# Where the transposes of a cosine attention and mixer kernel are made: DMA queue or TensorE

## The chip, the core and the metric

The kernel runs on one core of a Trainium2 chip. Its engines are TensorE (PE, matmuls; PEld is its weight load), VectorE (DVE), ScalarE (ACT), GpSimd (POOL) and SyncE (SP); 16 DMA engines serve the queues that SP and POOL issue to. The metric is the device time of one execution in microseconds (us); lower is better. The kernel before took 548.46 us (median of 3 runs, 548.42 to 548.52).

## The reference: what is computed

Attention with normalised queries and keys over 8 batches of 12 heads, 448 positions and 64 dimensions a head, and on its result a mixer with a low-rank step and a wide MLP:

```python
q_n = q / (norm(q) + 1e-06); k_n = k / (norm(k) + 1e-06)
attn = softmax(q_n @ k_n.T / tau)          # per batch and head
x = (attn @ v), heads joined               # [8, 448, 768]
u = x + (x.T @ U @ V).T                    # U [448, 32], V [32, 448]
out = u + relu(u @ w_ch1) @ w_ch2          # w_ch1 [768, 3072], w_ch2 [3072, 768]
```

## The kernel before, in words

**Order of the work.** The program first lists all work as `Op`s: engine, planned duration, what it depends on, which buffer slots it takes (`acq`) and gives back (`rel`). `Plan.run` then simulates the engines with these durations and sorts all operations by their planned start. Every engine executes its instructions in that fixed order on the chip; nothing is reordered there. PE's operations stand in streams with a rank: of the streams whose next operation is ready, the first listed one goes (transposes `pe_tp` before attention products `pe_av`, scores `pe_sc` after them, and the MLP `pe_mlp` last, as what fills PE). An operation of PE is planned only 0.1 us (`SEM`) and a margin (`plan.safe`: 0.2 us while batch 1 is listed, 0.5 us for batches 2 to 7) after the end of what it depends on. A DMA on the queue of SP is planned as 0.1 us of issue, its work on one shared line ("x"; 1.0 us for a store of u) and a fixed delay (2.0 us for it). `"ACT/DVE"` means that whichever of the two is free takes the operation.

**Attention.** For each batch b = 0 to 7 and each of 6 head pairs, q and k come in by POOL's queue, are squared and summed (`squares`, L641 to L649), and scaled on DVE (`norm`, L717) into a tile `xn` of 112 rows with 8 blocks of 128 columns (4 of k, 4 of q, two heads side by side). The scores need each block transposed, `qkT`, in the tile that the profile calls sqk. In batches 0 and 1 (`PE_BATCHES = 2`) the function `flip` (L559 to L580) does that on PE: transposes with `ident` (the matmul at L571) into one PSUM bank, then one copy to SBUF by ACT (L1446) or DVE (L1448). In batches 2 to 7 one DMA transpose for the pair, issued by SP (L733), takes the place of both. Scores (L781) follow in bursts of three slots that take pairs of the PSUM banks 0 to 5, exponentials on ACT (L799), products with v (L826), and a scaling on DVE (L857, L858) into X, of which there are two buffers, one for the even and one for the odd batches. `LAST` says at which pair the scores of the last 64 keys of pairs 0, 2 and 4 (and of the pair after each) are made in batches 2 to 7.

**u.** `stage0` projects X with U (L941), multiplies with V (L994) and adds that to X in place (L1003). Two batches together make seven tiles of 128 rows, named (z, t) with z = b // 2; tile t = 3 holds 64 rows of each batch, so each batch makes its half of it. A store on SP's queue (L1032) writes each tile to DRAM, `kept[x]`. For batch 0's tiles and tile (0, 3) the columns (the transposed u, which the MLP needs) are made on PE and never leave the chip.

**The MLP.** `mlp` handles the first four tiles. The other 24 go in twelve host pairs: `columns_of` fetches for each tile the columns into the single buffer `uT` by a DMA transpose of `kept[x]` (L891) and the rows by a plain load (L895). `mlp_seven` then multiplies: the first six pairs at L1270 (up) and L1299 (down), the last six at L1163 (up, with sums of weights that L1122 to L1125 write into buffers which attention no longer needs, X among them) and L1299. Where the plan leaves PE idle for over 0.25 us, filler matmuls go in (L703).

Lines of note: `flip` L559, matmul L571; `squares` L627; `norm` with L733; `stage0` with L1032; `columns_of` with L891 and L895; copies of `copy_op` L1446 (ACT) and L1448 (DVE).

Of the kernel before, what the change touches and what calls it, by code (L numbers as in the profile page):

```python
# [317 lines left out]
def kernel(  # L318
# [31 lines left out]
    HALF = 6  # L350
    POOL_XN = {}
    WHOLE = 3
    LAST = {0: 0, 2: 2, 4: 5}
    WIDE = 1
    TB = 2
    RAW_KEYS = {(0, 0), (0, 1)}
# [48 lines left out]
    r_ur = Shrink([u_t[:, i, :] for i in range(3)], 3, (0, 1))  # L405
    dram = ctx.enter_context(tc.tile_pool(name="dram", bufs=1, space=bass.MemoryType.DRAM))
    kept = {(z, t): dram.tile([128, C], BF, name=f"u_{z}_{t}") for z in range(B // 2) for t in range(7) if (z, t) >= (0, 3)}
    uT_t = const.tile([128, CC * 512], BF, name="uT")
    r_uT = fixed_ring([uT_t])

# [53 lines left out]
    r_z = bank_ring([(7,), (4,), (6,), (5,), (3,), (1,), (2,), (0,)], 4)  # L464
    r_sc = bank_ring([(0, 1), (2, 3), (4, 5)], 3)
    r_low = bank_ring([(5,), (4,), (3,), (2,), (1,), (0,)], 4)
    r_av3 = bank_ring([(5,), (4,), (3,), (2,), (1,), (0,)], 2, (4, D + 8))
    r_av2 = bank_ring([(5,), (4,), (3,), (2,), (1,), (0,), (6,)], 2, (4, D + 8))
    r_up0 = bank_ring([(7,), (6,), (5,), (4,), (3,), (2,), (1,), (0,)], 3)
# [32 lines left out]
    pe_first = plan.stream("PE")  # L502
    pe_z2 = plan.stream("PE")
    pe_z1 = plan.stream("PE")
    pe_av = plan.stream("PE")
    pe_z0 = plan.stream("PE")
    pe_a = plan.stream("PE")
# [14 lines left out]
    def dve_t(n, fast=1, fixed=0.065):  # L522
        return fixed + n * 0.00105 / fast
# [32 lines left out]
            in_=moe_w_ch2.rearrange("(a p) c -> p a c", p=128)[:, i * w:(i + 1) * w, :]),  # L556
            C * w * 128 * 4 / 415e3)

    def flip(stream, ins, n, into, part, deps, acq, rel, wide=1, eng="ACT/DVE", took=0.05):  # L559


        tp = Slot(r_mm, 1)
        tp.own = True
        for z, x in enumerate(ins):
            def fn(z=z, x=x):
                if z == 0:
                    w = len(ins) // wide
                    tp.tile = bank_t[:, tp.group[0], :].bitcast(BF)[:, 0:w * n].rearrange(
                        "p (w n) -> p w n", w=w)
                m = 128 // wide  # L570
                nc.tensor.transpose(out=tp.tile[m * (z % wide):m * (z % wide + 1), z // wide, :], in_=x(),  # L571
                                    identity=ident[:n, :n])
            o = plan.add(Op("PE", took, fn, deps=deps + [id_set] if z == 0 else (), acq=[tp] + acq,
                            rel=rel if z == len(ins) - 1 else []), stream)
        took = any_t(n * len(ins) // wide, 2)
        c = plan.add(Op(eng, took, None, deps=[o], acq=acq, rel=[tp], prio=0.2, fast=True))

        def move():
            for dst, src in part(into(), tp.tile):
                copy_op(c, dst, src)  # L580
        c.fn = move
        return c
# [45 lines left out]
    def squares(b, g, ld, ops, lo, ii, ss, pr, on, hold, then):  # L628

        red = []  # L630
        for i in ii:
            for a0 in range(0, g, G // 2):
                a1 = min(g, a0 + G // 2)
                sq = Slot(r_sq, 1)
                o = Op(on, 1.02 if on == "POOL" else {"ACT": 0.52, "DVE": 0.34} if "/" in on else 0.52 if on == "ACT" else 0.34, None,
                       deps=[ops[i], *hold], acq=[sq], prio=pr + 0.2, fast=True, port=True)

                def square(o=o, i=i, a0=a0, a1=a1, sq=sq):
                    x, y = ld.tile[:, i, lo + a0:lo + a1, :], sq.tile[:, 0:a1 - a0, :]
                    if o.by == "ACT":  # L640
                        nc.scalar.activation(out=y, in_=x, func=AF.Square)  # L641
                    elif o.by == "POOL":
                        nc.gpsimd.tensor_mul(y, x, x)  # L643
                    else:
                        nc.vector.tensor_mul(y, x, x)
                o.fn = square
                plan.add(o, pool_q if on == "POOL" else None)
                red.append(plan.add(Op("DVE", dve_t(256 * (a1 - a0)),
                    lambda i=i, a0=a0, a1=a1, sq=sq: nc.vector.reduce_sum(  # L649
                        ss.tile[:, i, a0:a1, :].rearrange("p h c -> p (h c)"),  # L650
                        sq.tile[:, 0:a1 - a0, :].rearrange("p h (c d) -> p (h c) d", d=D),
                        axis=AX.X),
                    deps=[o, *then], acq=[ss], rel=[sq], prio=pr + 0.1)))
        return red
# [50 lines left out]
    def norm(b, p, ld, la, inv, a, deps, pr, loaded):  # L705


        by_pe = b < PE_BATCHES
        first = b == 0 and p == 0
        xn, qkT = Slot(r_xn, 2 if by_pe and (first or (b, p) not in RAW_KEYS) else 1), Slot(r_qkT, SC if b == 0 else sum(p in members(b, x) for x in groups_of(b)))  # L710

        def part(i):
            def fn():
                src = ld.tile[:, i, la:la + 2, :].rearrange("p h (c d) -> p h c d", d=D)
                sc = inv.tile[:, i, a:a + 2, :].unsqueeze(3).to_broadcast([SCH, 2, SC, D])
                dst = xn.tile[:, SC * (1 - i):SC * (2 - i), :].rearrange("p c (h d) -> p h c d", h=2)
                (nc.gpsimd if pool_ else nc.vector).tensor_mul(dst, src, sc)  # L717
            pool_ = i in POOL_XN.get(b, ())
            return plan.add(Op("POOL" if pool_ else "DVE", 1.05 if pool_ else dve_t(512), fn, deps=[deps[i]], acq=[xn],
                               rel=[getattr(ld, "slot", ld), inv], prio=pr, port=True), pool_x if pool_ else None)  # L720

        def raw():
            c = Op("ACT/DVE", any_t(512), None, deps=loaded[1], acq=[xn], rel=[ld.slot], prio=-0.9)
            c.fn = lambda: copy_op(
                c, xn.tile[:, 0:SC, :].rearrange("p c (h d) -> p h c d", h=2),
                ld.tile[:, 1, la:la + 2, :].rearrange("p h (c d) -> p h c d", d=D))
            return plan.add(c)

        keys = (b, p) in RAW_KEYS
        ops = {0: part(0), 1: raw()} if first and keys else {0: part(0)} if keys else {  # L730
            i: part(i) for i in ((0, 1) if first else (1, 0))}
        if not by_pe:
            done = [plan.add(Op("SP", 0.1, lambda: nc.sync.dma_start_transpose(  # L733
                out=qkT.tile, in_=xn.tile.rearrange("p b e -> p (b e)")), deps=list(ops.values()), acq=[qkT],
                rel=[xn], prio=0, lat=("x", 0.05 * 56, 5.0)))]
        else:
            done = []
            for i in (1, 0) if keys else ops:
                b0, b1 = SC * (1 - i), SC * (2 - i)
                ins = [(lambda z=z: xn.tile[:, z, :]) for z in range(b0, b1)] if i in ops else [  # L740
                    (lambda c=c, hh=hh: ld.tile[:, 1, la + hh, D * c:D * c + D]) for c in range(SC) for hh in range(2)]
                done.append(flip(
                    pe_tp, ins, SCH,
                    lambda: qkT.tile, (lambda t_, x, b0=b0, b1=b1: [(t_[:, b0:b1, :], x)]),
                    [ops[i]] if i in ops else loaded[1], [qkT], [xn if i in ops else ld], len(ins) // SC,
                    "ACT/DVE", 0.05))
        got[b, p, "qkT"] = (qkT, done, (inv, a, deps[1]))
        return list(ops.values())
# [123 lines left out]


    prev, first_v, made, u_adds, projects = {}, {}, {}, {}, {}

    class Columns:

# [7 lines left out]
    def columns_of(tiles, uses=NC * CC, given=None):  # L885
# [2 lines left out]
        us = []  # L888
        for i, x in enumerate(tiles):
            if given is None:  # L890
                ut.append(plan.add(Op("SP", 0.1, lambda i=i, x=x: nc.sync.dma_start_transpose(  # L891
                    out=uT.tile[:, :, i * 128:(i + 1) * 128], in_=kept[x]),
                    deps=made[x], acq=[uT.slot], prio=0, lat=("x", 0.05 * 48, 2.0))))
            u = Slot(r_ur, 2)
            u.back = plan.add(Op("SP", 0.1, lambda x=x, u=u: nc.sync.dma_start(out=u.tile, in_=kept[x]),  # L895
                                 deps=made[x], acq=[u], prio=1, lat=("x", 1.0, 2.0)))
            us.append(u)
# [31 lines left out]
    def stage0(b, X, muls):  # L929
# [95 lines left out]
        for i, t in enumerate(tiles):  # L1025
# [5 lines left out]
            made.setdefault(x, []).append(plan.add(Op(  # L1031
                "SP", 0.1, lambda x=x, r=r, t=t: nc.sync.dma_start(out=kept[x][r, :], in_=X.tile[r, t - 3 * par, :]),  # L1032
                deps=u_adds[x], rel=[X], prio=1 if b == 1 else 0, lat=("x", 1.0, 2.0))))
        prev["A"], prev["X"] = A, X
        return us, uT, ut

# [563 lines left out]
    for n in range(0, len(rest), 2):  # L1600
        if n // 2 == HALF:
            up = seven_rows([hosts[-1][0][-1]], [
                [o for t in range(4) for o in made[3, t][:1]]] * 2 + [
                [o for p in range(NPAIR) for o in got[B - 1, p, "qkT"][1]] if i in (2, 4) else
                [last_av[B - 1 if i == 6 else B - 2, p] for p in range(NPAIR)] for i in range(2, 7)])
            held = stores + [last_av[B - 1, p] for p in range(NPAIR)]
# [54 lines left out]
```

## Time and profile before

| what | value |
|---|---|
| median of 3 runs | 548.46 us |
| the profiled execution's own time | 547.75 us |
| its span, first to last instruction | 546.0 us |
| PE busy | 537.7 us, 98% |
| DVE busy | 448.7 us, 82% |
| ACT busy | 280.7 us, 51% |
| POOL busy | 141.8 us, 26% |
| DMA transposes of q and k (L733) | 36, 4.5 us from issue to landing (median) |
| DMA transposes of u (L891) | 24, 3.3 us |
| stores of u (L1032) | 28, 2.6 us |
| matmuls at L571 (transposes on PE) | 106 |

How to read the views that the prediction uses: the busy slices divide the span in 40 equal parts, a digit is the busy share in tenths, and PEclk is TensorE's granted clock in tenths. The chain of work that ended last, in order of time, has the start in us, the length in us, and the engine, tile and line, with the number of instructions. The waits have the waiting engine, tile and line, what released it, and then the total in us, the number of times and the longest. A row of the timeline begins with the start and the length in us of a group of like instructions that lie together. A row of one source line has the durations in ns (least, median, most) and the first and last start. The windows have, for a stretch, the busy us of each engine. The duration of a matmul runs from its start to its modelled end and overlaps the next one; the distance between the starts of two neighbours is called the pitch here.

### The profile page before, as it was taken

Reading aid. Unit: us, or ns where it says so; the run is one execution under the profiler, and the core shown is the slowest. Engines: PE = TensorE matmul, PEld = TensorE weight load, DVE = VectorE, ACT = ScalarE, POOL = GpSimd, SP = SyncE. Lnnn points to the kernel's source line nnn. Section 1 sums busy time; section 2 is a strip of 40 time slices with the busy share of each in tenths; the row PEclk is TensorE's granted clock in tenths of the full one; section 3 lists DMA queues with packets and bytes.
Section 4 is the critical chain, followed back from the end, with each engine's and each line's share of the span. In section 5 each row is a group of like instructions: output and inputs, shape, how many; then the busy total and the mean of one; then the engine's idle time right before and its main releaser. Section 6 shows DMA issues by size and latency. Waiting matters only on the chain.

```text
span 546.0 us, 15182 instructions
## 1 busy us (share of the span) xinstructions
PE 537.7 (98%) x6276; PEld 390.2 (71%) x6276; DVE 448.7 (82%) x1033; ACT 280.7 (51%) x459; POOL 141.8 (26%) x180
## 2 busy tenths in 40 slices
PE   8899999999999999999999999999999999999996
PEld 7565655677757857767757857868778787878783
DVE  8979949999899989979979976678968585858583
ACT  7977646466456746766765664732323231314140
POOL 8636233100711611631631610010202020111111
PEclk9999999999999999999999999999999999999999
DMA  9999999941985987998996975023041312122301
GB/s 156 202 207 141 206 203 159 199 88 47 140 190 102 121 140 145 135 141 136 137 154 102 133 138 92 32 53 87 16 139 30 88 32 88 30 88 32 88 1 59
DMA packets 142325, 61.11 MB, mean 112 GB/s; under 512 B 101008, under 2 KB 142256, under 8 KB 142256
## 3 DMA queue, kind: packets, MB, share of 16 engines
q0 software_dynamic: 72352, 25.73, 44.3%
q1 hardware_dynamic: 69904, 34.41, 29.1%
q8 instruction: 49, 0.80, 0.6%
q14 instruction: 20, 0.16, 0.1%
HBM read 56.93 MB, written 15.93 MB: 133 GB/s over the span
## 4 chain that ended last, share of the span: by engine, by line
PE 94%; DVE 3%; ACT 1%; POOL 1%; DMA 1%; issue 0%; DVEq 0%; POOLq 0%
PE bank L1299 30%; PE bank L1270 18%; PE bank L1163 15%; PE bank L826 8%; PE bank L781 7%; PE bank L1382 6%; PE bank L1424 6%; PE bank L994 2%; DVE qk_all L717 1%; PE bank L941 1%; DVE ss L649 1%; POOL sqk L643 1%; DMA relu<-in_q_dram 1%; PE bank L571 1%; DVE X_sb L864 0%; ACT attn L794 0%
## 5 line engine op out<-in xcount | busy, mean ns | idle before, releaser
L799 ACT ACTIVATE attn<-bank 128x896 bf16<-128x896 f32 (+1 forms) x163 | 139.1, 915 | 39.9 <-PE bank L781 34.0
L1299 PEld LDWEIGHTS <-relu 128*128 128x128 bf16 x1008 | 96.0, 98 | 67.1 <-issue 7.2
L1270 PE MATMUL bank<-uT,w_sb 128*128 128x256 bf16 x864 | 103.9, 273 | 0.0
L1299 PE MATMUL bank<-w_sb,relu 128*128 128x384 bf16 x576 | 101.9, 326 | 0.0
L1270 PEld LDWEIGHTS <-w_sb 128*128 128x128 bf16 x864 | 81.8, 98 | 18.7 <-issue 8.2
L649 DVE TENSOR_REDUCE ss<-sqk 112x8 f32<-112x512 bf16 x96 | 62.5, 676 | 2.7 <-ACT sqk L641 2.0
L717 DVE TENSOR_TENSOR qk_all<-qk_all,inv 112x512 bf16<-112x512 bf16 x93 | 60.7, 682 | 0.8 <-DMA sqk<-qk_all 0.5
L826 PEld LDWEIGHTS <-attn 128*128 128x128 bf16 (+1 forms) x1536 | 54.3, 97 | 6.6 <-issue 2.9
L593 POOL DMA_DIRECT2D qk_all<-in_q_dram x24 | 17.7, 736 | 155.4 <-ACT attn L799 76.9
L826 PE MATMUL bank<-v_nat,attn 128*128 128x65 bf16 (+1 forms) x1536 | 57.3, 193 | 0.6 <-DVE X_sb L864 0.6
L1163 PEld LDWEIGHTS <-w_sb 128*128 128x128 bf16 x864 | 49.3, 98 | 0.8
L1280 ACT ACTIVATE relu<-bank 128x512 bf16<-128x512 f32 x45 | 26.9, 597 | 42.2 <-PE bank L1270 42.0
L1200 ACT COPY attn<-bank 128x512 f32<-128x512 f32 x18 | 10.5, 587 | 74.1 <-PE bank L1163 73.2
L781 PE MATMUL bank<-sqk 64*64 64x448 bf16 (+1 forms) x460 | 46.9, 356 | 0.7 <-ACT sqk L1446 0.5
L1163 PE MATMUL bank<-uT,w_sb 128*128 128x128 bf16 x648 | 38.1, 219 | 0.0
L1191 ACT ACTIVATE relu<-relu 128x512 bf16<-128x512 bf16 x36 | 22.6, 630 | 29.9 <-DVE relu L1185 29.1
L616 POOL DMA_DIRECT2D v_nat<-in_v_dram x42 | 31.2, 759 | 18.6 <-DMA w_sb<-in_moe_w_ch_dram 14.9
L1382 PE MATMUL bank<-uT,w_sb 128*128 128x384 bf16 (+1 forms) x288 | 35.9, 273 | 0.0
L1424 PE MATMUL bank<-w_sb,relu 128*128 128x384 bf16 x192 | 35.1, 326 | 0.0
L641 ACT ACTIVATE sqk<-qk_all 112x512 bf16<-112x512 bf16 x47 | 28.7, 631 | 9.8 <-DVE ss L649 9.7
L858 DVE TENSOR_TENSOR X_sb<-bank,rd 128x256 bf16<-128x256 f32 x72 | 30.5, 424 | 2.5
L1003 DVE TENSOR_TENSOR X_sb<-bank,X_sb 128x384 bf16<-128x384 f32 (+3 forms) x57 | 29.0, 542 | 1.7 <-PE bank L994 1.2
(132 smaller groups left out, 799.7 us busy)
## 6 DMA issues: line engine op xcount, KB each, us to landing
qk_all<-in_q_dram POOLq DMA_DIRECT2D x23, 224.0 KB, 5.5
qk_all<-in_k_dram POOLq DMA_DIRECT2D x23, 224.0 KB, 6.3
u_nat<-u SPq DMA_DIRECT2D x25, 192.0 KB, 2.9
w_sb<-in_moe_w_ch_dram POOLq DMA_DIRECT2D x4, 1152.0 KB, 18.1
w_sb<-in_moe_w_ch_dram POOLq DMA_DIRECT2D x8, 576.0 KB, 15.4
u<-X_sb SPq DMA_DIRECT2D x22, 192.0 KB, 2.8
v_nat<-in_v_dram POOLq DMA_DIRECT2D x11, 168.0 KB, 8.6
out_dram<-O_sb SPq DMA_DIRECT2D x11, 168.0 KB, 2.8
```

Of the source, the lines that this page charges most:

```text
L616: ops = [load(lambda j=j, r0=r0, c=c, s0=s0, s1=s1: nc.gpsimd.dma_start(out=v_t[b % 2][r0:r0 + s1 - s0, :, j, 0:D], in_=src[c, s0:s1]), (s ...
L649: lambda i=i, a0=a0, a1=a1, sq=sq: nc.vector.reduce_sum(ss.tile[:, i, a0:a1, :].rearrange("p h c -> p (h c)"), sq.tile[:, 0:a1 - a0, :].re ...
L717: (nc.gpsimd if pool_ else nc.vector).tensor_mul(dst, src, sc)
L781: nc.tensor.matmul(out=out, lhsT=qkT.tile.rearrange("p b s -> p (b s)")[r, n0:n0 + w], rhs=qkT.tile[r, SC:2 * SC, :].rearrange("p c s -> p ...
L799: exps.append(plan.add(Op("ACT", act_t(2 * S, 0.058), lambda sc=sc, c=c, attn=attn: nc.scalar.activation(out=attn.tile[:, :, off:off + S] ...
L826: nc.tensor.matmul(out=av.tile[:, t, 0:D + 1], lhsT=tail.tile[:, hh, 128 * t:128 * (t + 1)] if tail and j == SC - 1 else (attn if j < SC - ...
L858: nc.vector.tensor_mul(X.tile[:, :, h * D:(h + 1) * D], av.tile[:, :, 0:D], rd.tile.to_broadcast([128, 4, D]))
L1163: o = plan.add(Op("PE", pe_t(128), lambda i=i, j=j, jj=jj: nc.tensor.matmul(out=mm.tile[:, 128 * jj:128 * jj + 128], lhsT=left[k](i, j), r ...
L1270: o = plan.add(Op("PE", pe_t(256), lambda j=j, e=e, cc=cc, mm=mm: nc.tensor.matmul(out=mm.tile[:, 256 * e:256 * e + 256], lhsT=w1_sb[:, cc ...
L1299: o = plan.add(Op("PE", pe_t(CH), lambda j=j: nc.tensor.matmul(out=mm.tile[:, 0:CH], lhsT=left[k](j), rhs=right[k](j), start=(first and j ...
L1382: o = plan.add(Op("PE", pe_t(n), lambda cc=cc: nc.tensor.matmul(out=mm.tile[:, m:m + n], lhsT=w1_sb[:, cc, f * 128:(f + 1) * 128], rhs=uT. ...
L1424: nc.tensor.matmul(out=mm.tile[:, 0:c1 - c0], lhsT=relu.tile[:, f, i * 128:(i + 1) * 128], rhs=w2_t[:, f, c0:c1], start=(f == 0), stop=(f ...
```

## The change

The DMA transposes go. For q and k, `norm` calls `flip` with all eight blocks of a pair: 8 transposes of 112 columns into one PSUM bank (of `r_low`, banks 0 to 5), one copy of 896 columns to `qkT`. For u, `stage0` calls `flip` on the tile in X after its store has been issued, and with that store among what it depends on: 6 transposes of 128 columns into one bank, one copy back into the same place in X (of the whole tile, or of 64 of each 128 columns for a half of tile 3). A second store writes this to a new DRAM tile, `turned[x]`, and `columns_of` fetches the columns from there with a plain load. The new PE stream `pe_u` ranks before the attention products. The weights' sums that overwrite X now also wait for the second store. Two more edits: `LAST` for pair 4 is 4 instead of 5, and in batch 0 the first square of two heads is split, one head on ACT and one on DVE.

```diff
--- before.py
+++ after.py
@@ -350,7 +350,7 @@
     HALF = 6
     POOL_XN = {}
     WHOLE = 3
-    LAST = {0: 0, 2: 2, 4: 5}
+    LAST = {0: 0, 2: 2, 4: 4}
     WIDE = 1
     TB = 2
     RAW_KEYS = {(0, 0), (0, 1)}
@@ -405,6 +405,7 @@
     r_ur = Shrink([u_t[:, i, :] for i in range(3)], 3, (0, 1))
     dram = ctx.enter_context(tc.tile_pool(name="dram", bufs=1, space=bass.MemoryType.DRAM))
     kept = {(z, t): dram.tile([128, C], BF, name=f"u_{z}_{t}") for z in range(B // 2) for t in range(7) if (z, t) >= (0, 3)}
+    turned = {x: dram.tile([128, C], BF, name=f"uT_{x[0]}_{x[1]}") for x in kept if x != (0, 3)}
     uT_t = const.tile([128, CC * 512], BF, name="uT")
     r_uT = fixed_ring([uT_t])
 
@@ -464,6 +465,7 @@
     r_z = bank_ring([(7,), (4,), (6,), (5,), (3,), (1,), (2,), (0,)], 4)
     r_sc = bank_ring([(0, 1), (2, 3), (4, 5)], 3)
     r_low = bank_ring([(5,), (4,), (3,), (2,), (1,), (0,)], 4)
+    r_fl = bank_ring([(5,), (4,), (3,), (2,), (1,), (0,), (6,)], 2)
     r_av3 = bank_ring([(5,), (4,), (3,), (2,), (1,), (0,)], 2, (4, D + 8))
     r_av2 = bank_ring([(5,), (4,), (3,), (2,), (1,), (0,), (6,)], 2, (4, D + 8))
     r_up0 = bank_ring([(7,), (6,), (5,), (4,), (3,), (2,), (1,), (0,)], 3)
@@ -502,6 +504,7 @@
     pe_first = plan.stream("PE")
     pe_z2 = plan.stream("PE")
     pe_z1 = plan.stream("PE")
+    pe_u = plan.stream("PE")
     pe_av = plan.stream("PE")
     pe_z0 = plan.stream("PE")
     pe_a = plan.stream("PE")
@@ -556,10 +559,10 @@
             in_=moe_w_ch2.rearrange("(a p) c -> p a c", p=128)[:, i * w:(i + 1) * w, :]),
             C * w * 128 * 4 / 415e3)
 
-    def flip(stream, ins, n, into, part, deps, acq, rel, wide=1, eng="ACT/DVE", took=0.05):
-
-
-        tp = Slot(r_mm, 1)
+    def flip(stream, ins, n, into, part, deps, acq, rel, wide=1, eng="ACT/DVE", took=0.05, ring_=None):
+
+
+        tp = Slot(ring_ or r_mm, 1)
         tp.own = True
         for z, x in enumerate(ins):
             def fn(z=z, x=x):
@@ -632,6 +635,19 @@
             for a0 in range(0, g, G // 2):
                 a1 = min(g, a0 + G // 2)
                 sq = Slot(r_sq, 1)
+                if b == 0 and g == 2 and i == 0 and len(ii) == 1:
+                    halves = [
+                        plan.add(Op("ACT", 0.31, lambda sq=sq: nc.scalar.activation(
+                            out=sq.tile[:, 0:1, :], in_=ld.tile[:, 0, lo:lo + 1, :], func=AF.Square),
+                            deps=[ops[i]], acq=[sq], prio=pr + 0.2)),
+                        plan.add(Op("DVE", 0.33, lambda sq=sq: nc.vector.tensor_mul(
+                            sq.tile[:, 1:2, :], ld.tile[:, 0, lo + 1:lo + 2, :], ld.tile[:, 0, lo + 1:lo + 2, :]),
+                            deps=[ops[i]], acq=[sq], prio=-9, port=True))]
+                    red.append(plan.add(Op("DVE", dve_t(512), lambda sq=sq: nc.vector.reduce_sum(
+                        ss.tile[:, 0, 0:2, :].rearrange("p h c -> p (h c)"),
+                        sq.tile[:, 0:2, :].rearrange("p h (c d) -> p (h c) d", d=D), axis=AX.X),
+                        deps=halves, acq=[ss], rel=[sq], prio=-9)))
+                    continue
                 o = Op(on, 1.02 if on == "POOL" else {"ACT": 0.52, "DVE": 0.34} if "/" in on else 0.52 if on == "ACT" else 0.34, None,
                        deps=[ops[i], *hold], acq=[sq], prio=pr + 0.2, fast=True, port=True)
 
@@ -730,9 +746,9 @@
         ops = {0: part(0), 1: raw()} if first and keys else {0: part(0)} if keys else {
             i: part(i) for i in ((0, 1) if first else (1, 0))}
         if not by_pe:
-            done = [plan.add(Op("SP", 0.1, lambda: nc.sync.dma_start_transpose(
-                out=qkT.tile, in_=xn.tile.rearrange("p b e -> p (b e)")), deps=list(ops.values()), acq=[qkT],
-                rel=[xn], prio=0, lat=("x", 0.05 * 56, 5.0)))]
+            ins = [(lambda z=z: xn.tile[:, z, :]) for z in range(2 * SC)]
+            done = [flip(pe_tp, ins, SCH, lambda: qkT.tile, lambda t_, x: [(t_, x)], list(ops.values()), [qkT], [xn],
+                         ring_=r_low)]
         else:
             done = []
             for i in (1, 0) if keys else ops:
@@ -872,6 +888,7 @@
 
 
     prev, first_v, made, u_adds, projects = {}, {}, {}, {}, {}
+    made_t = {}
 
     class Columns:
 
@@ -888,9 +905,10 @@
         us = []
         for i, x in enumerate(tiles):
             if given is None:
-                ut.append(plan.add(Op("SP", 0.1, lambda i=i, x=x: nc.sync.dma_start_transpose(
-                    out=uT.tile[:, :, i * 128:(i + 1) * 128], in_=kept[x]),
-                    deps=made[x], acq=[uT.slot], prio=0, lat=("x", 0.05 * 48, 2.0))))
+                ut.append(plan.add(Op("SP", 0.1, lambda i=i, x=x: nc.sync.dma_start(
+                    out=uT.tile[:, :, i * 128:(i + 1) * 128],
+                    in_=turned[x].rearrange("p (c n) -> p c n", c=CC)),
+                    deps=made_t[x], acq=[uT.slot], prio=0, lat=("x", 1.0, 2.0))))
             u = Slot(r_ur, 2)
             u.back = plan.add(Op("SP", 0.1, lambda x=x, u=u: nc.sync.dma_start(out=u.tile, in_=kept[x]),
                                  deps=made[x], acq=[u], prio=1, lat=("x", 1.0, 2.0)))
@@ -1031,6 +1049,17 @@
             made.setdefault(x, []).append(plan.add(Op(
                 "SP", 0.1, lambda x=x, r=r, t=t: nc.sync.dma_start(out=kept[x][r, :], in_=X.tile[r, t - 3 * par, :]),
                 deps=u_adds[x], rel=[X], prio=1 if b == 1 else 0, lat=("x", 1.0, 2.0))))
+            if x in turned:
+                X.uses += 1
+                X.left += 1
+                view = lambda t=t: X.tile[:, t - 3 * par, :].rearrange("p (c n) -> p c n", c=CC)
+                c = flip(pe_u, [(lambda cc=cc, t=t: X.tile[:, t - 3 * par, 128 * cc:128 * cc + 128]) for cc in range(CC)],
+                         128, view, lambda t_, y, r=r: [(t_[:, :, r], y[:, :, r])], u_adds[x] + made[x][-1:], [], [],
+                         took=0.056, ring_=r_sc1 if b == 1 else r_fl)
+                made_t.setdefault(x, []).append(plan.add(Op(
+                    "SP", 0.1, lambda x=x, r=r, view=view: nc.sync.dma_start(
+                        out=turned[x].rearrange("p (c n) -> p c n", c=CC)[:, :, r], in_=view()[:, :, r]),
+                    deps=[c], rel=[X], prio=1 if b == 1 else 0, lat=("x", 1.0, 2.0))))
         prev["A"], prev["X"] = A, X
         return us, uT, ut
 
@@ -1600,7 +1629,7 @@
     for n in range(0, len(rest), 2):
         if n // 2 == HALF:
             up = seven_rows([hosts[-1][0][-1]], [
-                [o for t in range(4) for o in made[3, t][:1]]] * 2 + [
+                [o for t in range(4) for o in made[3, t][:1] + made_t[3, t][:1]]] * 2 + [
                 [o for p in range(NPAIR) for o in got[B - 1, p, "qkT"][1]] if i in (2, 4) else
                 [last_av[B - 1 if i == 6 else B - 2, p] for p in range(NPAIR)] for i in range(2, 7)])
             held = stores + [last_av[B - 1, p] for p in range(NPAIR)]
```

## The prediction

> **What bounds the kernel now.** I read the busy slices of the page first, for an engine that never rests:
>
> ```profile
> PE   8899999999999999999999999999999999999996
> ...
> DVE  8979949999899989979979976678968585858583
> ACT  7977646466456746766765664732323231314140
> ...
> PEclk9999999999999999999999999999999999999999
> ```
>
> PE is full from the third slice (27 us) to the last but one, at the full granted clock. DVE is close to full up to slice 24 (about 330 us), ACT has a third to a half free, and nothing but PE is full after that. A busy PE need not be a fast one, so I looked next at the chain of work in order of time, near its end:
>
> ```profile
> 500.32 13.65 PE bank L1299 x84
> 513.97 14.07 PE bank L1163 x252
> ```
>
> 84 matmuls of 384 columns take 13.65 us, 162.5 ns each; 252 of 128 columns take 14.07 us, 55.8 ns each. A third of the columns takes a third of the time, so these matmuls stream without holes between them. The same pitches hold earlier: in the trace the median distance between two starts is 162 ns on L1299 and 109 ns on L1270 over the whole run, and distances more than 60 ns above the pitch of their shape add up to 5.3 us, 4.8 of them before 50 us. Last, the table of waits for PE alone, which is complete here:
>
> ```profile
> PE bank L703 <- DVE warm L1467: 1.1, 1, 1.1
> PE bank L571 <- DVE qk_all L717: 1.0, 2, 0.7
> PE bank L826 <- DVE X_sb L864: 0.6, 2, 0.4
> PE bank L571 <- DVE sqk L1448: 0.3, 1, 0.3
> PE bank L781 <- ACT sqk L1446: 0.5, 1, 0.5
> PE bank L781 <- ACT attn L794: 0.2, 1, 0.2
> ```
>
> 3.7 us in all, every one of them in batch 0 or 1 or in the start, and no DMA among them. So the end of the kernel is the sum of PE's pitches, and whatever is added to PE's stream after 30 us moves the end by its own pitch.
>
> **What is removed.** 36 DMA transposes of q and k (L733, batches 2 to 7, six pairs each) and 24 of u (L891). PE waited for neither: no row above names them. What goes is SP time (the issue of one takes 1.25 us on SP's queue, a plain DMA 0.36) and DMA traffic: the 256-byte packets of the transposes are 16% of the 16 engines' span. I cost this at **no gain**; at most it could return PE's waits after 88 us, where the first transpose stands, and those are about 0.5 us.
>
> **What PE gets.** Each of the 36 pairs now has 8 transposes of 112 columns: 288. Each u tile has 6 of 128 columns, made for batch 1 three times (tiles 4 to 6; tile 3 is excluded) and for batches 2 to 7 four times, since tile 3 is turned once for each of its halves: 27 x 6 = 162. Batches 0 and 1 run such transposes already, at L571, and the timeline shows their groups:
>
> ```profile
> 66.72 0.36 PE L571 MATMUL bank<-ident,qk_all 112*128 112x112 bf16 x4
> ...
> 69.29 0.76 PE L571 MATMUL bank<-ident,qk_all 112*128 112x112 bf16 x12
> ```
> ```profile
> 101.24 0.39 PE L571 MATMUL bank<-ident,X_sb 128*128 128x128 bf16 x4
> ```
>
> One alone takes 0.21 us, but the next starts long before it ends. (0.76 - 0.21)/11 = 0.050 us is the pitch of 112 columns, and (0.39 - 0.22)/3 = 0.057 of 128. Sum: 288 x 0.050 = 14.4, 162 x 0.057 = 9.2, together **23.6 us**. The change of shape costs nothing more: from an L1382 matmul to an L571 one and back the trace has the plain pitches, 162 and 49 ns. Bounds: 23.0 with 0.0485 and 0.0558; above, the full 0.21 us of each one, were none to overlap, 450 x 0.21 = 95. I take 23.6, as the groups are the same instructions.
>
> [...] This trace has 0.212 to 0.219 us for one but pitches of 50 and 57 ns, so the measured pitch decides. [...]
>
> **What ACT and DVE get.** One copy per pair (896 columns) and one per u flip (21 of 768, 6 of 384). ACT's rows of bf16 copies at L1446 are 0.375 us for 256 columns and 0.537 for 448, so 0.84 ns a column: 0.91, 0.81 and 0.48 us. DVE's row at L1448 is 0.385 us for 448; its float32 casts (0.555 for 384, 0.678 for 512) have 0.96 ns a column, so 896 lie between 0.60 and 0.82. All on ACT: 36 x 0.91 + 21 x 0.81 + 6 x 0.48 = 53 us. All on DVE: 40 to 50. Between 88 and 350 us the windows give
>
> ```profile
> sum 262.00, PE 262.00 PEld 186.06 DVE 234.15 ACT 162.58 POOL 69.31; mean PE 43.67 PEld 31.01 DVE 39.02 ACT 27.10 POOL 11.55
> ```
>
> so DVE has 28 us free and ACT 99, and the stretch itself grows by most of the 23.6. I cost the copies at **nothing**, under PE's own work. Were the cover gone, attention would run later, but MLP matmuls stand behind it in the stream, and tiles are made well ahead of their use: the seventh host pair (first L1163, 373.5 us) uses tiles stored between 261 and 298. The last attention product is at 363.9, and L1122 to L1125, which prepare that pair's operands, end at 376.9, so that is the tightest place; it moves back by the same PE work as what it follows.
>
> **The new wait.** PE used to wait for no DMA in mid-stream. Now the first transpose of each u flip waits until the store of that tile (L1032) has landed, because the copy overwrites X in place. Behind it on PE stand the attention products, the scores and the MLP in their fixed order, and with them ACT and DVE. The planner reckons 0.1 + 1.0 + 2.0 us for a store, 0.1 for the semaphore and a margin of 0.5 (0.2 in batch 1): 3.7 us from the add. What a store takes, from issue to landing:
>
> ```profile
> L1032 SPq DMA_DIRECT2D u<-X_sb x28: 332/363/973, 101.7 to 399.1; - x28
> ...
> DMA to landing us min/median/max: 1.9/2.6/7.4
> ```
>
> The median is inside, the longest ones are not: those beside q, k or v loads landed 4.17 us (151 us), 5.81 (223), 4.47 (252), 6.93 (267), 3.98 (304) and 7.41 (309) after their issue, and the four of batch 1 between 5.5 and 6.9. Over 3.7 the six are 10.6 us too long in sum. Batch 1's four queue behind one another, for which the planner allows 1 us each; I allow 2 us there. Upper bound 12.6 us if the landings stay. Lower bound 0, since the transposes that shared the DMA engines with these stores go and since the order shifts by some us. I take a third, **4 us**: the transposes are 87 us (16% of 546) of some 243 us that the windows from 88 to 350 us show the DMA engines busy, against which 51 plain transfers of at most 192 KB come, so fewer stores should land late.
>
> Smaller parts, all at nothing. The u tile's way is longer by a flip, a second store and a plain load in place of the transpose, about 2.6 + 1.5 us; the tightest user, the second host pair (up-projection at 168 us), had its last transpose landed at 158.4. The tail scores of the last pairs move from one burst to the one before, with the same matmuls. The first square is split over ACT and DVE: from 0.63 to about 0.42 us in the start, at most 0.2 us, if the later steps of the start, which also wait for POOL (L643) and loads, pass it on.
>
> **Sum.** The profiled execution took 547.75 us (span 546.0 and 1.75 around it). 547.75 + 23.6 + 4 = 575.35. The median of the runs shown, 548.46, is 0.7 above that execution, so I forecast **576.0**.
>
> **Rivals.**
> 1. *The store takes the place of the transpose.* PE stands at most of the flips until the store has landed. For: the ten long landings above, and PE's order can't be changed on the chip. Against: 18 of 28 were under 3.8 us. Price: 12.6 us as the landings stood, up to 28 if half the flips met the mean of those ten, 5.7 us (14 x 2.0). 548.5 + 23.6 + 12.6 = 585, to 600. It decides from a mean landing above 3.7.
> 2. *The pitch is partly free.* PE's filler and stalls of the first 30 us, or holes that the modelled ends hide, take some transposes in, so that about 10 to 20 us remain: 559 to 569. Against: the pitches scale with the columns, and no flip that is added lies before 88 us.
> 3. *Faster.* The DMA transposes now hold back something that PE waits for, between 88 us and the end, and their going returns more than 23.6 us. All of PE's idle time is 546.0 - 537.7 = 8.3 us, and most of it is before 30 us or after the last matmul. It decides only if more than 23.6 us of holes were hidden inside busy PE; then about 546. The equal pitches exclude nearly all of it.
> 4. *Nothing overlaps.* The transposes cost their full 0.21 us: 548.5 + 95 = 643. The groups of L571 speak against it.
>
> **How the numbers follow.** The forecast, 570 to 580: 0.62. Rival 1, above 580: 0.26. Rival 2: 0.08. Rival 3: 0.01. Rival 4: 0.02. No measurable change, which is within 0.2% (about what a measurement here can tell from none): 0.01. The range runs from 569.5 to 588: it holds the forecast and two thirds of rival 1, with the bounds of the new wait. Slower by over 0.2%: 0.62 + 0.26 + 0.08 + 0.02 = 0.98; same 0.01; faster 0.01.
>
> **What would show it.** In the profile after: about 550 matmuls at the line of the transposes, in groups with pitches of 50 and 57 ns; L1299, L1270 and L1163 at 162, 109 and 56 ns as before; PE busy over 97%. The new wait right: rows "PE (or its loads) <- DMA u<-X_sb" or <- the store, of some 4 us in sum. Rival 1: over 12 us there. Rival 3: fewer us in PE's stream between 88 and 350. The copies wrongly costed: waits of PE for ACT or DVE copies at the helper's lines, or DVE above 97% up to 350 us. The forecast falls if the PE stream grows by less than 20 or more than 28 us without waits.

## The result, and the profile after

The changed kernel took 574.02 us (median of 4 runs, 573.32 to 574.59) beside 548.44 us of the kernel before on the same chip: a ratio of 1.0466, 95% interval 1.0447 to 1.0484. It is slower by 25.6 us. The forecast was 576.0 us, the range 569.5 to 588. The profiled execution took 573.77 us with a span of 572.0 us, 26.0 us more than before.

The busy slices of the changed kernel, tenths of 40 equal parts:

```profile
PE   8899999999999999999999999999999999999996
...
DVE  8979859999898989979969976687897776758583
ACT  7977655766567874766865684560404141414140
...
PEclk9999999999999999999999999999999999999999
```

PE is as full as before at the same clock, in a longer span. The page has ACT busy for 306.2 us (before 280.7) and DVE for 464.3 (448.7): they have taken the copies. The chain near its end still shows both pitches unchanged, 162.5 ns and 55.8 ns (start, length, line, count):

```profile
526.29 13.65 PE bank L1328 x84
539.94 14.07 PE bank L1192 x252
```

(L1328 and L1192 are the old L1299 and L1163; the up-projection L1270 is now L1299, the matmul of `flip` L574.) The added transposes, as the row of that line and groups of the timeline have them:

```profile
L574 PE MATMUL bank<-ident,X_sb x168: 217/219/223, 101.9 to 428.5; 128*128 128x128 bf16 x168
```
```profile
145.20 0.55 PE L574 MATMUL bank<-ident,qk_all 112*128 112x112 bf16 x8
...
173.87 0.50 PE L574 MATMUL bank<-ident,X_sb 128*128 128x128 bf16 x6
```

(0.55 - 0.21)/7 = 0.049 us and (0.50 - 0.22)/5 = 0.056 us: the pitches of the forecast. All of PE's waits in the changed kernel:

```profile
PE bank L1299 <- ACT relu L1309: 1.4, 1, 1.4
PE bank L574 <- DVE qk_all L733: 1.4, 3, 0.7
PE bank L719 <- DVE warm L1496: 1.1, 1, 1.1
PE bank L842 <- DVE X_sb L880: 0.6, 2, 0.4
PE bank L797 <- ACT sqk L1475: 0.5, 1, 0.5
PE bank L574 <- DVE sqk L1477: 0.3, 1, 0.3
PE bank L797 <- ACT attn L810: 0.2, 1, 0.2
PE bank L1299 <- ACT attn L815: 0.2, 1, 0.2
PE bank L1012 <- issue: 0.2, 1, 0.2
PE bank L842 <- DVE X_sb L1021: 0.2, 1, 0.2
```

No row names a store or a DMA. One new row stands out, 1.4 us for a relu on ACT.

**Where the 26.0 us came from.** I summed, over the whole trace, the distance from the start of each matmul to the start of the next, by the line of the first. From PE's first matmul to its last end this is 540.6 us before and 566.6 us after:

| distance between starts, us | before | after | difference |
|---|---|---|---|
| transposes of 112 columns (100, then 388) | 5.77 | 19.95 | +14.18 |
| transposes of 128 columns (6, then 168) | 0.34 | 9.56 | +9.22 |
| up-projection, 256 columns (864) | 96.76 | 98.76 | +2.01 |
| down-projection, 384 columns (1008) | 165.95 | 166.42 | +0.47 |
| all else | 271.81 | 271.91 | +0.1 |

23.4 us are the transposes' own pitches, 2.6 us are gaps that were not there. Counting only gaps over 0.3 us after 88 us (a gap is what the distance has over the pitch), there were none before and there are three after: 0.32 us at 216.4, 0.34 at 316.9 and 1.55 at 328.3.

**The largest new gap**, in the timeline of the changed kernel:

```profile
325.36 0.50 PE L574 MATMUL bank<-ident,X_sb 128*128 128x128 bf16 x6
...
326.65 1.91 PE L1299 MATMUL bank<-uT,w_sb 128*128 128x256 bf16 x16
...
328.59 0.80 ACT L1475 COPY X_sb<-bank 128x768 bf16<-128x768 bf16 x1 [3.40 <-PE bank L1299]
...
329.29 0.60 ACT L1309 ACTIVATE relu<-bank 128x512 bf16<-128x512 f32 x1
...
329.94 0.60 PE L1299 MATMUL bank<-uT,w_sb 128*128 128x256 bf16 x4 [1.38 <-ACT relu L1309]
```

The six transposes of u ran at 325.36. The store of that tile, issued at 321.56 beside the loads of v, landed 6.96 us later, at 328.52. The copy overwrites what the store reads, so ACT stood 3.40 us and copied from 328.59. (The profile names PE as the releaser; it had long been done, and the landing 0.07 us earlier is what fits.) The relu queued behind the copy was late, its bank stayed taken, and PE waited for it. So the wait for the store is on the engine that copies, and not on PE: PE only reads X, as the store does, and its transposes started 3.16 us before the landing. Two more copies held ACT until a landing, 0.41 us at 226 and 0.61 us at 274, and PE felt neither.

### The profile page after: what moved, and what is told of

Its sections match the earlier page's. It is cut to its first block, busy times and chain, and to the rows that moved or that the text cites. A ratio compares the mean times of both kernels' runs of the same rounds, so it can differ in the third digit from the quotient of the medians.

```text
span 572.0 us, 16131 instructions
## 1 busy us (share of the span) xinstructions
PE 561.3 (98%) x6721; PEld 412.7 (72%) x6722; DVE 464.3 (81%) x1061; ACT 306.2 (54%) x495; POOL 148.5 (26%) x180
## 4 chain that ended last, share of the span: by engine, by line
PE 91%; DVE 5%; ACT 1%; DMA 1%; issue 1%; POOL 0%; SPq 0%; DVEq 0%; POOLq 0%
PE bank L1328 28%; PE bank L1299 16%; PE bank L1192 15%; PE bank L842 8%; PE bank L797 6%; PE bank L1411 6%; PE bank L1453 6%; PE bank L574 5%; DVE qk_all L733 2%; PE bank L1012 1%; DVE ss L665 1%; PE bank L959 1%; DMA relu<-in_k_dram 1%; DVE X_sb L1021 0%; DMA out_dram<-relu 0%
## 5 line engine op out<-in xcount | busy, mean ns | idle before, releaser
L1328 PEld LDWEIGHTS <-relu 128*128 128x128 bf16 x1008 | 95.5, 98 | 66.2 <-issue 7.7
L1299 PE MATMUL bank<-uT,w_sb 128*128 128x256 bf16 x864 | 106.1, 273 | 1.6 <-ACT relu L1309 1.4
L1328 PE MATMUL bank<-w_sb,relu 128*128 128x384 bf16 x576 | 103.4, 326 | 0.0
L1299 PEld LDWEIGHTS <-w_sb 128*128 128x128 bf16 x864 | 81.0, 98 | 20.3 <-issue 9.9
L1309 ACT ACTIVATE relu<-bank 128x512 bf16<-128x512 f32 x48 | 28.7, 598 | 44.1 <-PE bank L1299 43.3
L1192 PEld LDWEIGHTS <-w_sb 128*128 128x128 bf16 x864 | 49.3, 98 | 0.8
L1229 ACT COPY attn<-bank 128x512 f32<-128x512 f32 x18 | 10.6, 587 | 65.6 <-PE bank L1192 60.6
L1192 PE MATMUL bank<-uT,w_sb 128*128 128x128 bf16 x648 | 38.1, 219 | 0.0
L1353 POOL TENSOR_TENSOR relu<-relu,u_nat 128x384 f32<-128x384 f32 x7 | 8.4, 1205 | 110.0 <-ACT relu L1351 82.7
L1453 PE MATMUL bank<-w_sb,relu 128*128 128x384 bf16 x192 | 35.4, 326 | 0.0
L1353 POOL TENSOR_TENSOR attn<-attn,u_nat 128x384 f32<-128x384 f32 x6 | 12.8, 2156 | 69.0 <-ACT attn L1351 69.0
## 6 DMA issues: line engine op xcount, KB each, us to landing
w_sb<-in_moe_w_ch_dram POOLq DMA_DIRECT2D x8, 576.0 KB, 15.5
```

Of the source, the lines that this page charges most:

```text
L1192: o = plan.add(Op("PE", pe_t(128), lambda i=i, j=j, jj=jj: nc.tensor.matmul(out=mm.tile[:, 128 * jj:128 * jj + 128], lhsT=left[k](i, j), r ...
L1299: o = plan.add(Op("PE", pe_t(256), lambda j=j, e=e, cc=cc, mm=mm: nc.tensor.matmul(out=mm.tile[:, 256 * e:256 * e + 256], lhsT=w1_sb[:, cc ...
L1328: o = plan.add(Op("PE", pe_t(CH), lambda j=j: nc.tensor.matmul(out=mm.tile[:, 0:CH], lhsT=left[k](j), rhs=right[k](j), start=(first and j ...
L1453: nc.tensor.matmul(out=mm.tile[:, 0:c1 - c0], lhsT=relu.tile[:, f, i * 128:(i + 1) * 128], rhs=w2_t[:, f, c0:c1], start=(f == 0), stop=(f ...
```

## The experiments

Times are medians; "before" was run beside each on its chip (548.05 to 548.39 us). Gaps are those over 0.3 us after 88 us, in the profiled execution. The edits are against the changed kernel unless said otherwise; `...` marks lines left out.

**Each part alone, and the transposes doubled.** *u alone*: `norm` keeps its DMA transposes.

```diff
-            ins = [(lambda z=z: xn.tile[:, z, :]) for z in range(2 * SC)]
-            done = [flip(pe_tp, ins, SCH, lambda: qkT.tile, lambda t_, x: [(t_, x)], list(ops.values()), [qkT], [xn],
-                         ring_=r_low)]
+            done = [plan.add(Op("SP", 0.1, lambda: nc.sync.dma_start_transpose(
+                out=qkT.tile, in_=xn.tile.rearrange("p b e -> p (b e)")), deps=list(ops.values()), acq=[qkT],
+                rel=[xn], prio=0, lat=("x", 0.05 * 56, 5.0)))]
```

> Only u is turned on TensorE; q and k of batches 2 to 7 go by DMA transposes as before (the two small edits are in). Pitch theory: 162 transposes x 0.057 us = 9.2 us, and the 2.6 us of new PE gaps of the changed kernel if they come from the u copies, which wait for the store of the tile: 557.6 to 560.3 us. Rival, the copies on ScalarE and VectorE set the time: 27 of the 63 copies, so about 43% of 25.6 us, 559.5, with waits of TensorE for copies and not for late landings. Rival, the stores' waits and nothing else: at most a few us over 548.4.

Measured: 562.33 us (560.31 to 563.05), ratio 1.0247 (1.0230 to 1.0264). The transposes took 9.6 us of PE, but the gaps were 4.5 us, more than either theory had. The largest, 2.09 us, follows a wait of VectorE's scaling for a DMA transpose of q and k to give its input buffer back; VectorE had no pause from there to the relu that PE waited for:

```profile
230.43 0.69 DVE L733 TENSOR_TENSOR qk_all<-qk_all,inv 112x512 bf16<-112x512 bf16 x1 [1.64 <-DMA sqk<-qk_all]
...
234.37 0.81 PE L1299 MATMUL bank<-uT,w_sb 128*128 128x256 bf16 x6 [1.92 <-DVE relu L1311]
```

*q and k alone*: `columns_of` keeps its DMA transposes and `stage0` makes no flips.

```diff
-                ut.append(plan.add(Op("SP", 0.1, lambda i=i, x=x: nc.sync.dma_start(
+                ut.append(plan.add(Op("SP", 0.1, lambda i=i, x=x: nc.sync.dma_start_transpose(
...
-            if x in turned:
+            if False and x in turned:
...
```

> Only q and k of batches 2 to 7 are turned on TensorE; u goes by DMA transposes as before (the two small edits are in). Pitch theory: 288 x 0.049 = 14.2 us and no new gaps, as no copy waits for a store here: 562.3 to 563.2 us, with executions as close together as the kernel before's. Rival, copies set the time: 36 of 63 copies, 57% of 25.6 us, also 563, but then with waits of TensorE for copies or scores. Rival, DMA transposes gone give something back: below 562.

Measured: 561.98 us (561.53 to 562.42), ratio 1.0249 (1.0234 to 1.0265). The sum over PE's starts grew by 13.8 us, 14.14 of it the transposes; no gap at all. 36 copies of 896 columns are fully covered. The median lies just under the 562 of the rival that the missing DMA transposes give something back, but the sum over PE's starts leaves them 0.3 us at most. This order has no gaps, so the new ones came with the u flips (in u alone the largest began at a DMA transpose of q and k).

*The two small edits alone*, `LAST` and the split square, with both parts of the change undone as above:

> The two small edits alone (tail scores of pair 4 at pair 4, the first square split over two engines); all transposes as before. Forecast's theory: at most 0.2 us off the start, 548.2 to 548.45 us. Rival, the edits hide a part of the transposes' cost or add to it: more than 0.5 us off 548.44 either way.

Measured: 549.52 us (548.82 to 549.73), ratio 1.0018 (1.0010 to 1.0027): about 1 us slower, and not 0.2 faster. One gap of 0.74 us at 194.0 came up, in an order without a single flip of u. The rival was right in this.

*Each added transpose twice*:

```diff
-                nc.tensor.transpose(out=tp.tile[m * (z % wide):m * (z % wide + 1), z // wide, :], in_=x(),
-                                    identity=ident[:n, :n])
+                for _ in range(2 if ring_ else 1):
+                    nc.tensor.transpose(out=tp.tile[m * (z % wide):m * (z % wide + 1), z // wide, :], in_=x(),
+                                        identity=ident[:n, :n])
...
```

(The line left out plans them twice as long.)

> The changed kernel with each of the added 450 transposes issued twice into the same place; copies, stores and loads stay. Pitch theory: another 288 x 0.049 + 162 x 0.057 = 23.4 us, 597 to 598.5 us. Rival, the transposes fall partly into holes and the copies or the stores' waits are what costs: under 10 us more, below 584. Rival, each costs its full 0.21 us: 95 us more, 669.

Measured: 605.59 us (605.48 to 606.20), ratio 1.1044 (1.1029 to 1.1059), so 31.6 us over the changed kernel and not 23.4. PE's starts: 24.8 us more on the transposes (15.73 and 9.04). Most of the rest has a row of its own, the columns of u that came too late for the first and the second host pair:

```profile
PE bank L1300 <- DMA uT<-uT: 6.0, 2, 3.8
```

and a granted clock of 0.5 for 6.8 and 3.4 us with those two gaps (3.96 and 2.35 us), worth up to 5.1 us. The pitch is confirmed (24.8 with some of it at the low clock); the full 0.21 us of each transpose and the "holes" are both ruled out. The late columns were in neither theory.

**What makes the gaps.** *Flips later*: the first store of u is planned 3 us longer, so that no u copy stands before its store has landed.

```diff
-                deps=u_adds[x], rel=[X], prio=1 if b == 1 else 0, lat=("x", 1.0, 2.0))))
+                deps=u_adds[x], rel=[X], prio=1 if b == 1 else 0, lat=("x", 1.0, 5.0))))
```

> The changed kernel, with the first store of u planned 3 us longer, so that the flips of u stand later in the orders of all engines; the instructions are the same. Theory, the 2.6 us of new gaps come from u copies that ScalarE or VectorE hold until a late store has landed: 571.4 to 572.5 us, executions closer together than the 1.3 us of the changed kernel, no TensorE wait for a relu. Rival, the gaps come from the copies' own length or from the banks: 574 as before, within 0.6.

Measured: 574.10 us (573.81 to 574.75), ratio 1.0475 (1.0461 to 1.0489). No u copy was held by a landing any more (the nearest starts 0.4 us after one), and the sum over PE's starts had again grown by 26.0 us, so 2.6 us of gaps, at other places: 172 to 174, 267.6 and 277.4 us. There PE waits to get a PSUM bank for a flip of u, or for results behind the u copies:

```profile
172.86 0.50 PE L574 MATMUL bank<-ident,X_sb 128*128 128x128 bf16 x6 [0.28 <-DVE relu L1346]
...
173.73 0.50 PE L574 MATMUL bank<-ident,X_sb 128*128 128x128 bf16 x6 [0.37 <-ACT attn L815]
...
174.53 1.13 PE L842 MATMUL bank<-v_nat,attn 128*128 128x65 bf16 x32 [0.31 <-ACT attn L815]
```

So the late store explains the gap at 328 us of the one order, and an order without held copies has as much in gaps. My theory, that they are the whole cause, fell.

*Copies made twice* (and planned twice as long):

```diff
...
-            for dst, src in part(into(), tp.tile):
+            for dst, src in part(into(), tp.tile) * (2 if ring_ else 1):
```

> The changed kernel with each of its 63 copies out of PSUM made twice (and planned twice as long), some 40 us more of ScalarE and VectorE time; the transposes stay. Forecast's theory, the copies are covered: 574 to 577 us. Rival, ScalarE and VectorE bound the attention part: 10 us or more on top, from 584.

Measured: 585.62 us (585.06 to 587.05), ratio 1.0686 (1.0671 to 1.0700): 11.6 us more than the changed kernel for some 40 us of copies, in the rival's range. Gaps of 11.4 us in all:

```profile
PE bank L1301 <- DVE X_sb L1479: 2.4, 1, 2.4
PE bank L799 <- DVE X_sb L876: 2.1, 1, 2.1
PE bank L844 <- ACT attn L817: 1.9, 2, 1.8
PE bank L1194 <- DVE attn L1155: 1.8, 1, 1.8
```

and twice 3.4 us at half clock. The first row is a late store again, and not the copies' length: VectorE held a u copy until a landing, and PE stood for the bank that this copy frees.

```profile
241.89 1.15 DVE L1479 COPY X_sb<-bank 128x768 bf16<-128x768 bf16 x2 [2.26 <-DMA u<-X_sb]
...
243.09 0.60 PE L1301 MATMUL bank<-uT,w_sb 128*128 128x256 bf16 x4 [2.41 <-DVE X_sb L1479]
```

That gap (2.57 us) and the 3.4 us at half clock behind it, up to 1.7 us, are some 4 of the 11.6 us. The cover is real but thin: a second set of copies is covered for at least 70%. The last of the four rows is the place that the prediction called the tightest, the weights' sums before the seventh host pair.

*Copies planned as long as they are*, alone and with the later flips; and *all u copies on VectorE* (the line left out gives them VectorE's planned length):

```diff
+        if ring_:
+            took = {"ACT": 0.165 + n * len(ins) * 0.00083, "DVE": 0.165 + n * len(ins) * 0.0005}
```
```diff
...
-                         took=0.056, ring_=r_sc1 if b == 1 else r_fl)
+                         took=0.056, eng="DVE", ring_=r_sc1 if b == 1 else r_fl)
```

> The changed kernel with the 63 added copies planned as long as the profile shows them (VectorE 0.61 us for 896 columns in place of 0.54, ScalarE 0.91 in place of 0.80); the instructions are the same, their order may shift. Theory, the orders run ahead of ScalarE and VectorE, and TensorE's 2.6 us of new gaps come from that: about 572, gaps under 1.2 us. Rival, the gaps come from late stores alone: 573.5 to 574.5, with a gap behind a copy that waits for a store.

> Both at once: copies planned as long as they are, and the first store of u planned 3 us longer. If late stores and copies planned too short are the only sources of the new gaps: 548.4 + 23.4 = 571.8, to 572.4 us, gaps under 0.5 us. If the gaps belong to any order in which ScalarE and VectorE are this full: 573.5 or more.

> The changed kernel with all 27 copies of u on VectorE (0.55 us each, against 0.80 on ScalarE), so that a copy that waits for its store holds VectorE and never ScalarE with its exponentials and relus. If only what is queued behind the held copy matters, VectorE being the fuller engine: as slow or slower, 574 to 576. If ScalarE's queue is what TensorE waits for: below 573.

Measured: 578.52 us (576.11 to 580.07), 577.41 (577.08 to 579.10) and 578.89 (577.43 to 579.52), ratios 1.0553 (1.0533 to 1.0573), 1.0546 (1.0532 to 1.0561) and 1.0560 (1.0545 to 1.0574). All three slower than the changed kernel and outside what any theory had but "573.5 or more", with gaps of 3.7, 4.4 and 5.3 us, the largest of them between 173 and 178 us, where four flips of u, the up-projection of the second host pair and the columns for it come together. The columns came too late there in all three; the row of the first run:

```profile
PE bank L1301 <- DMA uT<-uT: 0.9, 1, 0.9
```

Telling the plan the truth about the copies didn't help, which speaks against the theory that its orders run ahead. With the copies on VectorE a late store held VectorE instead (1.30 us at 234, 1.82 at 282, 1.40 at 331), with gaps of PE behind it, so ScalarE's queue is nothing special. The six orders without doubled work (the changed kernel, the later flips, these three and the next run) have gaps of 2.2 to 5.3 us, of three kinds: a copy held by a late store (none with the later flips), a bank or a result that ACT or DVE hand over late, and late columns of u. That every order with ACT and DVE this full must have some is argued, not shown.

*The changed kernel without the small edits* (the first square as before, too):

```diff
-    LAST = {0: 0, 2: 2, 4: 4}
+    LAST = {0: 0, 2: 2, 4: 5}
...
```

> The changed kernel without the two small edits (tail scores of pair 4 at pair 5 as before, the first square on one engine). If the 1.1 us that the two cost alone is theirs wherever they stand: 572.9 us. Rival, that 1.1 us was one unlucky order: anything within 1 us of 574.0, with gaps of TensorE at other places.

Measured: 573.84 us (573.43 to 574.46), ratio 1.0468 (1.0453 to 1.0482), gaps of 2.5 us at 173.8, 175.3, 232.8 and 368.4. The rival holds: the small edits' 1.1 us was one order's. The largest gap, 1.10 us, is a wait for the second host pair's columns.

**The opposite of the change**, on the kernel before: q and k of batch 1 too go by DMA.

```diff
-        by_pe = b < PE_BATCHES
+        by_pe = b < 1
```

> The kernel before with the opposite of the change: q and k of batch 1 too go by DMA transposes, so TensorE has 48 transposes fewer. Pitch theory: 48 x 0.049 = 2.4 us less, 546.1 us, if none of the six lands late. Rival, they land late beside the weight loads, for which the DMA engines are busy in this part: TensorE waits for scores, 548.4 us or more.

Measured: 561.25 us (560.33 to 561.61), ratio 1.0234 (1.0221 to 1.0248): 12.9 us slower, though PE had 2.5 us fewer transposes. Batch 1 is worked on while the weights stream in. The rows of the DMA transposes and of PE's waits in this run:

```profile
L733 SPq DMA_TRANSPOSE sqk<-qk_all x42: 1222/1240/8346, 46.6 to 344.9; - x42
...
DMA to landing us min/median/max: 2.9/4.7/19.2
```
```profile
PE bank L1424 <- DMA w_sb<-in_moe_w_ch_dram: 4.0, 3, 2.9
PE bank L781 <- DMA sqk<-qk_all: 2.8, 1, 2.8
```

The last four of batch 1 landed 13.7, 19.2, 18.2 and 17.3 us after their issue, where all of the kernel before take 2.9 to 8.7, and one blocked SP for 8.3 us. The last of the eight loads of w_ch2 landed at 83.7 us, before at 76.9. PE stood 9.3 us in all between 60 and 125 us (6.8 of them until a DMA had landed, before none), and the clock was halved twice for 6.8 us, up to 6.8 us more: -2.5 + 9.3 + 6.8 = 13.6, against 13.5 in PE's sum. Plain DMAs were slow there as well: the loads of q and k issued beside them, at 59 and 63 us, took 26.4 and 24.1 us (the same two loads in the kernel before: 20.4 and 19.0).

## Why the prediction was right, point by point

- **PE's stream sets the end, and every added pitch moves it.** Right. Predicted 23.6 us, measured 23.4; the doubled transposes cost 24.8 more.
- **The removed DMA transposes give nothing back.** Right: with q and k alone on PE, the sum over PE's starts grew by 13.8 us, for 14.1 us of transposes.
- **The copies are covered.** Right for q and k. Too simple for the sum over 262 us from which it was read: DVE's 28 us and ACT's 99 us of free time aren't where four u tiles are turned within a few us (173 to 178), and a second set of copies cost 11.6 us, some 4 of them by a late store.
- **"Now the first transpose of each u flip waits until the store of that tile (L1032) has landed."** Wrong. That dependency stands in the plan only. On the chip the wait fell on the copy (ACT stood 3.40 us until 328.59), and PE felt it through the relu queued behind the copy (1.38 us). The term was 4 us and the gaps measured 2.6 us, but that the size came near is luck. The reason for taking only a third, that fewer stores would land late without the DMA transposes, failed as well: outside batch 1 seven stores landed later than 3.7 us after their issue, 18.5 us over it in sum, where the prediction had counted six with 10.6 us. They cost little because PE felt only one of them: 1.55 us of the 2.6 stood behind a held copy. The gaps at 216.4 and 316.9 us, 0.66 us together, were ended by results of DVE and ACT; what the remaining 0.4 us are stays open. In other orders the parts are others, and which need of the u flips (bank, copy, second store) weighs most stays open: a buffer of its own for the turned u, which would take the store's wait away, was not tried.
- **The longer way of the u tile, costed at nothing.** Right here, with no room left: the second host pair's columns landed at 173.27 us and its first matmul started at 173.31, where the kernel before had 158.43 and 166.3. In four other orders PE stood 0.4 to 0.9 us for them, and with the transposes doubled 6.0 us for two host pairs.
- **The small edits cost nothing.** Alone they cost 1.1 us, in the changed kernel nothing that can be told apart (573.84 against 574.02 us).
- **Rivals.** The store's wait on PE, the free pitch, the gain and the full 0.21 us each: none came as it was described. The error of the wait (4 against 2.6 us) is most of the distance from 576.0 to 574.0.

## What to carry to other kernels

PE's instructions stood pitch to pitch to the end here, and the 450 added transposes cost their pitch (0.049 and 0.056 us each, 23.4 us in all) and not their duration (0.21 us each). On the DMA queue the same work was all but free: taking q and k off it gave back 0.3 us at most. It was free by its place: six DMA transposes more cost 13 us where the weights were loading, so ask for each transpose what is full at that time. And the wait that the program planned for, of PE for the store, wasn't the wait that the chip made: the copy, which overwrites what the store reads, stood 3.40 us. So look which instruction overwrites something.

## What the runs showed of the hardware

The granted clock fell to one half, for 3.4 or 6.8 us, after short gaps of PE. In the rows of windows (start and end, length, then busy us and number of instructions by engine; PEclk is the third number from the right), of the run with the true copy lengths:

```profile
174.00:179.00 5.00, 2.86 (x52) 1.96 (x50) 4.86 (x13) 3.27 (x4) 0.00 (x0) 1.00 0.47 128
179.00:182.40 3.40, 3.40 (x22) 2.58 (x21) 1.70 (x4) 1.41 (x2) 3.00 (x5) 0.51 0.61 77
```

and of the run with batch 1 on DMA:

```profile
113.20:120.00 6.80, 5.80 (x53) 4.54 (x53) 5.38 (x13) 4.95 (x10) 0.00 (x0) 0.50 1.02 224
```

Gaps of 1.27 and 1.00 us within 3 us were followed by it (true lengths), as were 2.57 us (copies twice) and 1.45, 0.33 and 0.61 us within 4 us (u on VectorE, mean granted clock 0.996); 2.09 us alone (u alone) and 1.27 and 0.96 us (true lengths and later flips) were not (mean granted clock 1.0 in both). What tells them apart is not shown.

An estimate from these rows: a gap of 2.6 us in a full PE, as in the run with the copies made twice, can cost up to 4.3 us, itself and half of the 3.4 us at half the clock.
